# Attention, two MLPs, one core: no draining steps after the first batch, three buffers for its q and k, splits two steps ahead, M's last rows last in the first x2

## The chip, the cores and the metric

One core of a Trainium2 chip. The metric is device time in microseconds of one execution, the median over runs. TensorE (PE) multiplies matrices into PSUM, VectorE (DVE) and ScalarE (ACT) read PSUM and SBUF, GpSimd (POOL) works on SBUF, and the DMA queue of SyncE (SP) carries the transfers.

## The reference, cut to what matters

4 batches of 8 heads, 576 positions, head size 64; then 2304 rows through two blocks.

```python
scores = scale * np.matmul(q, k.transpose(0, 1, 3, 2))
s_pos = np.maximum(s, 0.0)
cum = np.cumsum(s_pos, axis=-1)
bias = -(cum[:, :, :, None] - cum[:, :, None, :])
scores = np.where(causal, -1000000000.0, scores + np.minimum(bias, 0.0))
attn = softmax(scores)                    # row maximum, exp, sum + 1e-9
x = np.matmul(attn, v)                    # heads side by side: (2304, 512)
a = x @ w1                                # (2304, 1024)
b = x @ w2
x2 = ((a * b) @ w3) @ w_out               # (2304, 512)
h = x2 @ w_in                             # (2304, 1024)
solu = h * softmax(h)
ln = (solu - mean) / sqrt(var + 1e-06) * g_ln
out = ln @ w_out2                         # (2304, 512)
```

## The kernel before

A number that needs more than one pass of TensorE is held as two parts, a high and a low one (`hi`, L90, and `lo`, L96), and a product is three matmuls (high by high, high by low, low by high). The weights come as 64-bit words in pieces of 128 x 512. `stage` loads a piece (two buffers during attention, four later), `to_f32` makes one 32-bit number of the two words (POOL or ScalarE at L369 or L371, then VectorE at L375, L376 and L379), and `split_w` writes the high part on ScalarE and the low part on VectorE or POOL (L97). This is a conversion; `pump(n)` runs n of them from a list.

The first loop goes over steps. Step `st` has a head `h` to score and a head `ph` to finish, two heads behind. Scoring is `qk_part` 0 to 2: matmuls of q and k (`sc`), VectorE adds the mask and takes the row extremes (L205), ScalarE takes the exponential (L209); `normalise` has VectorE take the reciprocals (L236, L237) and POOL scale the rows (L241). Finishing is `tr_part` 0 to 3, transposes by TensorE (L273 to L281) with copies out of PSUM into PT by ScalarE and VectorE in turn (L92, L94), and, for every second head, `av_parts`: attention times v (L305) into the tiles xT of its batch. Heads 0 to 7, the first batch, use plain 32-bit q and k in two pairs of buffers QN and KN (L183); later heads use parts, made by `split_qk` (ScalarE copies to QB and KA, VectorE casts to QA, POOL subtracts for QA and KB), with buffers QB, KB, QA and KA for two heads; L191 and L192 are their matmuls. `load_head` and `load_aug` issue the loads of a head and of its two extra rows on SP.

Before the change the steps are: heads 0 to 7; then two steps that score nothing and finish heads 6 and 7; then heads 8 and 9, which finish nothing; then the rest, 36 steps in all. From step 10 on, units of the first MLP (`ab_unit`: 12 matmuls for a and 12 for b of half a column block, L333, a copy of a by ScalarE, a product by VectorE, L353) are put between the parts of the steps as filling, `NF` of them in a step; the units of a batch need all of its xT. `PUMP` says how many conversions of w1 and w2 a step runs; unit i of a batch needs conversions 2i and 2i + 1. From step 11 on PSUM is dealt out anew. The `av_parts` of pairs up to head 9 run at once at the end of their step, the later ones one step late, among the filling.

Then the last units run, then M = w3 w_out is made row block by row block (`m_unit`, L595, high part MH by ScalarE, low part ML by VectorE) beside the conversions of w_in. Then x2 = g M for chunks of 256 rows: `x2_unit(c, *ms)` takes the column groups ms (of four), for each over the first seven row blocks of M, then over the eighth. The first chunk is done one column group at a time, and four conversions of the second w_out stand between the first and the second group. Then `h_unit`, `tr2` (L727) and `out_unit` follow for 18 tiles of 128 rows.

The order of the instructions on each engine is not that of the program: a planner (`schedule_with_timeline_sim=True`) orders them by the program's order as priority and its own estimate of when each is ready. Each engine then runs its own list in order.

## Time and profile before

| | us |
|---|---|
| median of 3 runs (802.27 to 805.4) | 804.95 |
| the profiled execution, device time | 808.67 |
| its span, first to last instruction | 806.9 |
| TensorE busy | 768.1 |
| VectorE busy | 461.1 |
| ScalarE busy | 350.1 |
| POOL busy | 261.5 |

TensorE's busy time is the time in which at least one matmul is under way; with a lower granted clock the same matmuls take longer, so a stretch is read by busy time and clock together. The mean granted clock was 0.979 of full speed. Busy times of VectorE contain the time in which an instruction was held up after its start. An idle time in brackets is that of the engine just before an instruction, with the instruction that ended it.

### The profile page before, as it was taken

What the parts mean: (1) busy time and instruction counts of PE and PEld (TensorE: products, weight loads), DVE (VectorE), ACT (ScalarE), POOL (GpSimd) and SP (SyncE); (2) the same over time, 40 slices, a digit from 0 to 9 for tenths busy, and PEclk for the clock granted to TensorE, in tenths of its full rate; (3) what the DMA queues carried; (4) which work ended last, traced back from release to release, by engine and by line L of the source; (5) the groups of instructions that cost most, each with busy time, mean ns of one, the idle gap of its engine ahead of it and who ended that gap; (6) DMA issues with size and microseconds to landing.
All of it is one profiled execution on the core that took longest, in us unless ns stands there. A gap on an engine that the chain in (4) does not pass through costs nothing.

```text
span 806.9 us, 13174 instructions
## 1 busy us (share of the span) xinstructions
PE 768.1 (95%) x4864; PEld 656.5 (81%) x4864; DVE 461.1 (57%) x1058; ACT 350.1 (43%) x847; POOL 261.5 (32%) x339
## 2 busy tenths in 40 slices
PE   7998979999999999999989969799999999999997
PEld 4555878788888888898988858788888888888886
DVE  5897698866454444325976899834344243433231
ACT  3763556576555464322435335624233232422231
POOL 8655568876544553102322344400000000000000
PEclk9998999999999999999999979899999999999999
DMA  5633355334323320104658644122020200000001
GB/s 149 179 111 98 114 169 164 106 94 130 87 79 104 90 75 31 45 30 170 239 167 281 210 160 139 72 66 66 14 66 14 66 26 14 14 14 14 14 27 39
DMA packets 38040, 75.59 MB, mean 94 GB/s; under 512 B 6796, under 2 KB 18060, under 8 KB 37976
## 3 DMA queue, kind: packets, MB, share of 16 engines
q1 hardware_dynamic: 37976, 74.76, 30.0%
q8 instruction: 38, 0.62, 0.3%
q14 instruction: 26, 0.21, 0.1%
HBM read 60.36 MB, written 14.38 MB: 93 GB/s over the span
## 4 chain that ended last, share of the span: by engine, by line
PE 72%; DVE 10%; DMA 8%; POOL 4%; issue 3%; ACT 2%; SPq 0%; ACTq 0%; DVEq 0%; POOLq 0%
PE o L738 13%; PE h L689 11%; PE x L669 10%; PE b L333 10%; PE a L333 9%; PE av L305 6%; PE tr L273 4%; DMA stage<-in_w_dram 3%; DVE stage L376 2%; PE sc L183 2%; DVE stage L375 2%; PE tr L727 2%; PE sc L191 2%; PE sc L192 2%; DVE stage L379 2%
## 5 line engine op out<-in xcount | busy, mean ns | idle before, releaser
L209 ACT ACTIVATE P<-P,STAT 64x64 f32<-64x64 f32 (+4 forms) x160 | 88.2, 553 | 58.4 <-DVE STAT L205 56.5
L241 POOL TENSOR_SCALAR P<-P,STAT 128x576 f32<-128x576 f32 (+4 forms) x160 | 89.7, 579 | 31.9 <-DVE STAT L237 29.9
L711 POOL TENSOR_TENSOR sv<-sv,mhalf 128x1 f32<-128x1 f32 x18 | 10.0, 555 | 262.2 <-DVE sv L708 262.2
L669 PE MATMUL x<-gh,MH 128*128 128x256 f32 x288 | 84.0, 292 | 5.8 <-ACT MH L92 5.8
L697 DVE TENSOR_REDUCE sv<-h 128x1 f32<-128x1024 f32 x18 | 22.0, 1224 | 115.1 <-PE h L689 115.1
L205 DVE CUSTOM_DVE_ANT_0 P<-sc,wmask 64x64 f32<-64x64 f32 (+4 forms) x160 | 71.7, 482 | 22.8 <-PE sc L192 13.9
L669 PE MATMUL x<-gh,ML 128*128 128x256 f32 x288 | 82.3, 286 | 2.2 <-DVE ML L97 2.2
L669 PE MATMUL x<-gl,MH 128*128 128x256 f32 x288 | 82.2, 286 | 0.0
L97 POOL TENSOR_TENSOR QA<-qk,QB 64x576 fp32r<-64x576 f32 x24 | 36.0, 1498 | 86.1 <-ACT QB L92 72.8
L333 PE MATMUL b<-xT0h,W 128*128 128x288 f32 x256 | 60.8, 309 | 3.2 <-DVE g_sb L353 3.2
L371 POOL TENSOR_SCALAR stage<-stage 128x512 f32<-128x512 f32 x40 | 32.2, 804 | 95.1 <-PE b L333 37.2
L669 PEld LDWEIGHTS x<-gh,MH 128*128 128x128 f32 x288 | 56.3, 195 | 7.1 <-ACT MH L92 6.3
L333 PE MATMUL b<-xT1h,W 128*128 128x288 f32 x256 | 59.2, 302 | 2.1 <-ACT a_sb L345 1.2
L94 DVE COPY PT<-tr 64x128 f32<-64x128 f32 (+5 forms) x112 | 41.2, 383 | 32.2 <-PE tr L281 11.0
L333 PE MATMUL a<-xT0h,W 128*128 128x288 f32 x256 | 59.2, 304 | 0.0
L689 PE MATMUL h<-IH,x2l 128*128 128x512 f32 x144 | 56.7, 394 | 1.5 <-DVE x2l L97 1.5
L333 PE MATMUL a<-xT1h,W 128*128 128x288 f32 x256 | 58.1, 300 | 0.0
L669 PEld LDWEIGHTS x<-gh,ML 128*128 128x128 f32 x288 | 56.0, 195 | 2.5 <-DVE ML L97 2.4
L353 DVE TENSOR_TENSOR g_sb<-b,a_sb 128x288 f32<-128x288 f32 x64 | 28.8, 452 | 50.9 <-PE b L333 25.3
L305 PE MATMUL av<-PT,vr 64*64 64x64 f32 (+4 forms) x384 | 57.2, 412 | 0.3 <-DVE PT L94 0.3
L738 PE MATMUL o<-OH,lh 128*128 128x512 f32 x144 | 57.1, 397 | 0.4 <-ACT lh L92 0.4
L738 PE MATMUL o<-OH,ll 128*128 128x512 f32 x144 | 57.0, 396 | 0.0
(124 smaller groups left out, 2032.5 us busy)
## 6 DMA issues: line engine op xcount, KB each, us to landing
stage<-in_w_dram SPq DMA_DIRECT2D x32, 512.0 KB
qk<-in_qk_dram SPq DMA_DIRECT2D x48, 288.0 KB
g_scr<-g_sb SPq DMA_DIRECT2D x32, 288.0 KB
stage<-in_wo_dram SPq DMA_DIRECT2D x16, 512.0 KB
graw<-g_scr SPq DMA_DIRECT2D x6, 1024.0 KB
out_dram<-o SPq DMA_DIRECT2D x18, 256.0 KB
vr<-in_vm_dram SPq DMA_DIRECT2D x16, 256.0 KB
stage<-in_w_in_dram SPq DMA_DIRECT2D x8, 512.0 KB
```

Of the source, the lines that this page charges most:

```text
L94: eng.tensor_copy(out=dst, in_=src)
L97: eng.tensor_tensor(out=dst, in0=src, in1=hi_.bitcast(F32), op=ALU.subtract)
L205: nc.vector.tensor_tensor_reduce(out=dst2, in0=ps_in, in1=msk, scale=-SCALE, scalar=BIG, op0=ALU.add, op1=ALU.min, accum_out=st[0:rows, ti ...
L209: nc.scalar.activation(out=dst, in_=dst, func=AF.Exp, bias=st[0:rows, ti:ti + 1], scale=-1.0, accum_out=st[0:rows, 5 + ti:6 + ti],)
L241: nc.gpsimd.tensor_scalar(out=dst, in0=dst, scalar1=r, scalar2=1.0, op0=ALU.mult, op1=ALU.mult)
L273: nc.tensor.transpose(ps[:, c:c + 128], pt[:, QOF[i] + 128 * j:QOF[i] + 128 * j + 128], ident)
L305: nc.tensor.matmul(st["ps"][64 * e:64 * e + 64, 448 + c0:448 + c1], vr[0:rows, j, e], PT[(2 * p + e) % 4][0:rows, o + c0:o + c1], **kw,)
L333: nc.tensor.matmul(ps, w_[:, c, fs], x_[:, c, sl], start=(c == 0 and w_ is WH and x_ is XH), stop=(c == KC - 1 and w_ is WL),)
L371: eng.tensor_scalar(out=high.bitcast(F32), in0=high.bitcast(F32), scalar1=2.0 ** -112, scalar2=1.0, op0=ALU.mult, op1=ALU.mult,)
L669: nc.tensor.matmul(ps[m], w_[:, k, m * 128:m * 128 + 128], g_[:, k], start=(k == 0 and w_ is MH and g_ is GH), stop=(k == KF - 1 and w_ is ...
L689: nc.tensor.matmul(ps[:, hf], x_[:, k, ts_], w_[:, k, hf * 512:hf * 512 + 512], start=(k == 0 and x_ is XH and w_ is IH), stop=(k == KC - ...
L738: nc.tensor.matmul(ps, l_[:, k], w_[:, k], start=(k == 0 and l_ is LH and w_ is OH), stop=(k == KF - 1 and l_ is LL),)
```

## The change

It takes the two steps that score nothing out of the list of steps: head h is scored in step h, head h - 2 finished in it, 34 steps in all. The units are two in each step from 10 on, the conversions are dealt to other steps (16 in all, as before), PSUM is dealt out anew at step 10 instead of 11, and the last pair of every batch is multiplied with v at once. The first batch gets a third pair of q and k buffers, made of a buffer of the tag qk2, set up by VectorE with three memsets and loaded ahead of the first score; a head's load is issued three heads ahead, its split done two heads ahead. In the first x2 all four column groups run together: first seven row blocks of M for all of them, then the eighth, with two of the groups in the halves of a two-bank PSUM tile; the four conversions of the second w_out come after all of it.

```diff
-            nc.sync.dma_start(out=QN[h % 2][64:128], in_=qkT[b, hh, :, 0])
-            after[0] = nc.sync.dma_start(out=KN[h % 2][64:128], in_=qkT[b, hh, :, 1])
+            nc.sync.dma_start(out=QN[h % 3][64:128], in_=qkT[b, hh, :, 0])
+            after[0] = nc.sync.dma_start(out=KN[h % 3][64:128], in_=qkT[b, hh, :, 1])
...
-    WO2 = (0, 4, 0, 0, 0, 2, 2)
-    XMS = ((0,), (1,), (2,), (3,))
+    WO2 = (0, 4, 2, 2)
+    XMS = ((0, 1, 2, 3),)
...
     for i in range(min(NQ, 2)):
         load_aug(i, cum[i:i + 1])
-    if NQ > 2:
-        nc.sync.dma_start(out=cumf_scr, in_=cum)
+
+    qk3 = at.tile([128, 2, S], F32, tag="qk2", bufs=2, name="qk3")
+    QN.append(qk3[:, 0])
+    KN.append(qk3[:, 1])
+    nc.vector.memset(qk3[0:64], 0.0)
+    nc.vector.memset(qk3[0:2, 0], 1.0)
+    nc.vector.memset(qk3[32:34, 1], -1.0)
+    load_head(2)
+    load_aug(2, cum[2:3])
+    nc.sync.dma_start(out=cumf_scr, in_=cum)
...
-    steps = [(h, h - 2 if h >= 2 else None) for h in range(H)]
-    steps += [(None, H - 2), (None, H - 1)]
-    steps += [(h if h < NH else None, h - 2 if h >= H + 2 else None) for h in range(H, NH + 2)]
-    NF = {10: 3, 11: 0, 12: 3, 13: 0, 14: 3, 15: 2, 16: 2, 17: 0, 18: 1, 19: 1, 20: 1, 21: 2, 22: 2, 23: 2, 24: 2, 25: 2, 26: 2, 27: 2, 28: 2, 29: 2, 30: 2, 31: 2, 32: 2, 33: 2, 34: 3, 35: 3}
-    PD, AVO = 10, 2
-    PUMP = {3: 1, 5: 1, 6: 1, 10: 2, 11: 1, 12: 2, 13: 1, 14: 3, 15: 2, 16: 1, 17: 1}
+    steps = [(h if h < NH else None, h - 2 if h >= 2 else None) for h in range(NH + 2)]
+    NF = {st: 2 for st in range(10, NH + 2)}
+    PD, AVO = 8, 2
+    PUMP = {4: 1, 6: 1, 8: 1, 9: 1, 10: 1, 11: 2, 12: 1, 13: 2, 14: 1, 15: 2, 16: 2, 17: 1}
...
-        if st == 11:
+        if st == 10:
             ps_ctx.close()
...
-            if NQ <= h + 2 < NH:
-                load_head(h + 2)
+            if NQ <= h + 3 < NH:
+                load_head(h + 3)
             qk_part(h, 0)
...
-            if h + 1 < NH:
-                split_qk(h + 1)
-            if h < 2 and h + 2 < NQ:
+            if h < 2:
                 aug_rows(QB[h], KB[h])
-            if h + 2 < NH:
-                if h + 2 < NQ:
-                    load_head(h + 2)
-                load_aug(h + 2, cumf_scr[h + 2:h + 3] if h + 2 < NQ else cum_scr[h + 2])
+            if h + 3 < NQ:
+                load_head(h + 3)
+                load_aug(h + 3, cumf_scr[h + 3:h + 4])
+            if NQ <= h + 2 < NH:
+                split_qk(h + 2)
+                load_aug(h + 2, cum_scr[h + 2])
         F(4)
         if ph is not None and ph % 2:
             parts = av_parts(ph // 2)
-            if ph < PD or st == len(steps) - 1:
+            if ph < PD or ph % H == H - 1:
...
-        ps = {m: smalltile("x2")[:, 0:256] for m in ms}
+        if len(ms) == KC:
+            two = bigtile("x2")
+            ps = {m: smalltile("x2")[:, 0:256] if m < 2 else two[:, m - 2, 0:256] for m in ms}
+        else:
+            ps = {m: smalltile("x2")[:, 0:256] for m in ms}
```

## Rows read from the trace of the kernel before

**Rows 1.** The page's totals: engine, busy us (share of the span), instructions.

```profile
PE 768.1 (95%) x4864; PEld 656.5 (81%) x4864; DVE 461.1 (57%) x1058; ACT 350.1 (43%) x847; POOL 261.5 (32%) x339
```

**Rows 2.** Stretches: stretch, length, then PE, PEld, DVE, ACT, POOL busy, clock, DMA, GB/s.

```profile
8.00:57.60 49.60, 44.42 (x221) 27.89 (x222) 39.49 (x128) 32.11 (x99) 32.21 (x55) 0.93 0.54 150
...
57.60:81.00 23.40, 19.60 (x116) 12.06 (x115) 17.02 (x35) 10.31 (x30) 13.27 (x17) 0.85 0.39 117
...
81.00:178.00 97.00, 89.80 (x651) 78.18 (x651) 75.93 (x197) 59.37 (x166) 67.91 (x76) 0.98 0.46 134
...
220.00:260.00 40.00, 40.00 (x300) 34.24 (x299) 18.93 (x65) 20.05 (x58) 18.12 (x25) 1.00 0.37 104
...
460.00:500.00 40.00, 30.55 (x185) 27.66 (x184) 37.13 (x52) 16.70 (x30) 18.52 (x16) 0.87 0.44 143
...
500.00:540.00 40.00, 35.83 (x206) 31.95 (x205) 27.36 (x50) 19.33 (x35) 11.87 (x12) 0.91 0.31 99
```

**Rows 3.** Timeline from 0 to 22: start, us, engine, line, operation, [idle before <-releaser].

```profile
0.88 0.30 DVE L447 MEMSET zz<- 128x288 f32 x1
...
8.13 6.32 PE L183 MATMUL sc<-KN,QN 128*128 128x288 f32 x24 [1.20 <-DMA KN<-cum]
...
9.49 0.76 DVE L205 CUSTOM_DVE_ANT_0 P<-sc,wmask 128x576 f32<-128x576 f32 x1 [2.56 <-PE sc L183]
...
14.60 5.08 POOL L241 TENSOR_SCALAR P<-P,STAT 128x576 f32<-128x576 f32 x10 [0.90 <-DVE STAT L237]
...
16.99 4.87 PE L183 MATMUL sc<-KN,QN 128*128 128x288 f32 x12 [2.54 <-DMA KN<-in_qk_dram]
```

**Rows 4.** Timeline around 37 to 42: POOL, VectorE, TensorE.

```profile
37.01 2.55 POOL L241 TENSOR_SCALAR P<-P,STAT 128x576 f32<-128x576 f32 x5
...
37.07 3.63 DVE L376 SCALAR_TENSOR_TENSOR stage<-stage 128x512 uint32<-128x512 uint32 x1 [1.44 <-POOL stage L371]
...
41.62 1.78 PE L183 MATMUL sc<-KN,QN 128*128 128x320 f32 x4 [2.29 <-DVE PT L94]
```

**Rows 5.** Stretches of line L375 alone: stretch, length, busy (count), clock, DMA, GB/s.

```profile
8.00:57.60 49.60, 2.99 (x5) 0.93 0.54 150
...
57.60:81.00 23.40, 2.71 (x3) 0.85 0.39 117
...
81.00:178.00 97.00, 9.99 (x8) 0.98 0.46 134
```

**Rows 6.** Tile stage, 8 to 180 us: ns min/median/max of VectorE's three lines.

```profile
L375 DVE TENSOR_SCALAR stage<-stage x16: 411/724/3003, 23.2 to 141.9; 128x512 uint32<-128x512 uint32 x16
...
L376 DVE SCALAR_TENSOR_TENSOR stage<-stage x16: 652/677/3631, 24.5 to 145.3; 128x512 uint32<-128x512 uint32 x16
...
L379 DVE SCALAR_TENSOR_TENSOR stage<-stage x16: 673/678/1894, 26.8 to 147.7; 128x512 uint32<-128x512 uint32 x16
```

**Rows 7.** Timeline around 58 to 64, the draining.

```profile
58.37 2.79 DVE L94 CAST QA<-qk 64x576 fp32r<-64x576 f32 x1
...
63.56 0.31 PE L277 MATMUL tr<-ident,P 64*64 64x64 f32 x1 [2.97 <-DVE PT L94]
```

**Rows 8.** Chain that ended last, two steady steps: start, us, engine, what, line.

```profile
203.41 3.15 PE av L305 x24
...
207.36 1.60 PE a L333 x12
...
226.65 3.15 PE av L305 x24
```

**Rows 9.** Timeline of TensorE around 100, in the second batch.

```profile
99.53 0.40 PE L191 MATMUL sc<-KB,QB 128*128 128x288 f32 x1 [0.71 <-POOL KB L97]
...
103.54 0.61 PE L333 MATMUL b<-xT0h,W 128*128 128x288 f32 x1 [3.21 <-DVE g_sb L353]
```

**Rows 10.** Timeline of TensorE around the first x2 and tile 0.

```profile
477.88 0.58 PE L669 MATMUL x<-gh,MH 128*128 128x256 f32 x1 [3.19 <-ACT MH L92]
...
514.61 1.97 PE L727 MATMUL tr<-ident,so 128*128 128x128 f32 x8 [4.17 <-DVE so L712]
```

More of the change, by code (lines that the diff above doesn't have):

```diff
@@ L111, in tile_attention_moe @@
         KO.append(KO[-1] + S - 128 * j)
-    QN = [at.tile([128, S], F32, tag="QA", bufs=2, name=f"QN{i}") for i in range(min(NQ, 2))]
-    KN = [at.tile([128, S], F32, tag="KA", bufs=2, name=f"KN{i}") for i in range(min(NQ, 2))]
+    QN = [at.tile([128, S], F32, tag="QA", bufs=2, name=f"QN{i}") for i in range(2)]
+    KN = [at.tile([128, S], F32, tag="KA", bufs=2, name=f"KN{i}") for i in range(2)]
     PT = [at.tile([128, KO[5]], F32, name=f"PT{i}") for i in range(4)]
@@ L147, in load_aug @@
         if h < NQ:
-            nc.sync.dma_start(out=QN[h % 2][32:33], in_=src)
-            nc.sync.dma_start(out=KN[h % 2][0:1], in_=src)
+            nc.sync.dma_start(out=QN[h % 3][32:33], in_=src)
+            nc.sync.dma_start(out=KN[h % 3][0:1], in_=src)
             return
@@ L183, in qk_mm @@
                 nc.tensor.matmul(
-                    view, QN[h % 2][:, q0:q0 + rows], KN[h % 2][:, c0:c0 + view.shape[-1]],
+                    view, QN[h % 3][:, q0:q0 + rows], KN[h % 3][:, c0:c0 + view.shape[-1]],
                     start=True, stop=True,
@@ L454, in tile_attention_moe @@
     load_head(0)
-    if NQ >= 1:
-        load_head(1)
+    load_head(1)
     cum = at.tile([NH, 2, S], F32, tag="qk2", bufs=2, name="cum")[:, 0]
@@ L467, in tile_attention_moe @@
     for i in range(2):
-        if i < NQ:
-            aug_rows(QN[i], KN[i])
-        if i + 2 >= NQ:
-            aug_rows(QB[i], KB[i])
+        aug_rows(QN[i], KN[i])
     nc.vector.tensor_scalar(out=s_sb, in0=s_sb, scalar1=0.0, scalar2=1.0 / SCALE, op0=ALU.max, op1=ALU.mult)
     nc.vector.tensor_tensor_scan(out=cum, data0=s_sb, data1=zero, initial=0.0, op0=ALU.add, op1=ALU.add)
-    for i in range(min(NQ, 2)):
+    for i in range(2):
         load_aug(i, cum[i:i + 1])
-    if NQ > 2:
-        nc.sync.dma_start(out=cumf_scr, in_=cum)
+    qk3 = at.tile([128, 2, S], F32, tag="qk2", bufs=2, name="qk3")
[7 more added lines that the diff above has]
+    nc.sync.dma_start(out=cumf_scr, in_=cum)
     hi(CK[:, 0], cum, nc.vector)
     lo(CK[:, 1], cum, CK[:, 0])
-    for i in range(NQ, 2):
-        load_aug(i, CK[i:i + 1])
     nc.sync.dma_start(out=cum_scr.bitcast(F32), in_=CK.bitcast(F32))
@@ L492, in tile_attention_moe @@
             nc.gpsimd.memset(t[64:128, KO[j]:KO[j] + 64], 0.0)
-    split_qk(0)
-    if NQ < 1:
-        load_head(1)
     nc.sync.dma_start(out=gln, in_=g_ln.rearrange("(k p) -> p k", p=128))
@@ L809, in tile_attention_moe @@
         if t < 2:
-            wo2_pump(WO2[5 + t])
+            wo2_pump(WO2[2 + t])
         if 0 <= t - 2 < NT:
```

## The prediction

> **What bounds the kernel now.** I read the totals first: TensorE is busy 768.1 of 806.9 us [rows 1], so the change can win only where TensorE stands still or runs slowly. Then the table of stretches: in each I call loss the length less TensorE's busy time times its granted clock [rows 2]. The first batch, 8 to 57.6 us: 49.6 - 44.42 x 0.93 = 8.3 us lost. The draining, 57.6 to 81: 23.4 - 19.60 x 0.85 = 6.7. The second batch up to the last weight conversions, 81 to 178: 97 - 89.8 x 0.98 = 9.0. Between 220 and 260 nothing is lost: TensorE 40.0 of 40 at clock 1.00, VectorE only 18.93. Around the first x2, 460 to 500 and 500 to 540: 13.4 and 7.4 by the same working. So 24 us of loss lie in front and 21 around x2, and in all of them VectorE is busy 68 to 93%: it is the second bound.
>
> Last, the waits. They name VectorE again and again, and behind it POOL: an L376 on VectorE ran 3.63 us from 37.07 while POOL worked on from 37.01 (the median of that line is 0.68), and TensorE stood for 2.29 us until 41.62 [rows 4, 6]. A 2.79 us cast for head 9's split at 58.37 was followed by a 2.97 us wait of TensorE at 63.56 [rows 7]. The orders on the engines are the planner's, not the program's: that cast stood ahead of transposes' copies of step 8, so all below assumes that the planner keeps its manner.
>
> **The change, part by part.** The profiled execution took 808.67 us for a span of 806.9. It is 3.7 us above the median of 804.95; I make the sum in its rows and take it off the median.
>
> *Third q and k.* TensorE scores heads 0 and 1 in 6.32 us (3.16 a head), waits 2.54 us for head 2's load and then takes 4.87 us for it [rows 3]. With a third buffer the load is issued before any score. It removes 2.54 us, and at most 4.87 - 3.16 = 1.71 more. Next late is POOL's normalising of head 0: ten instructions in 5.08 us from 14.60, five done near 17.1, while TensorE would be through with head 2 at 14.45 + 3.16 = 17.6. So it holds: -3.5 us, from -4.2 to 0. Added are three memsets on VectorE. The nearest row, 0.30 us for 288 columns, makes 1152 + 576 + 576 columns 2.4 us; VectorE idles for 2.56 us before its first score row at 9.49 [rows 3], which hides them. Without that cover they would cost their 2.4 us once. SP gets head 2's two loads and two small rows ahead of the two copies of cum; nobody needs those before head 3.
>
> *Fewer conversions in the first batch.* Before, 5 weight conversions had begun by 57.6 us and 8 of the 16 by 81 [rows 5]; the new PUMP asks for 2 in steps 0 to 7 and 4 by step 9. One costs VectorE 0.72 + 0.68 + 0.68 = 2.08 us at the medians [rows 6], some 2.4 with half of the low parts (an estimate: one more pass of 0.68, every second time). Fewer of them mean fewer cases like the one at 37.07, where TensorE has no a and b matmuls to fill with. I take -2 us, the wait of 2.29; from -3 to 0, since the planner may still hoist them.
>
> *No draining steps.* Steps 8 and 9 now score heads 8 and 9 beside the transposes of 6 and 7, without a and b. Two steady steps last 226.65 - 203.41 = 23.24 us [rows 8], 11.62 each, with two units of four matmul groups of 1.60: attention alone is 11.62 - 6.4 = 5.2 us of TensorE. VectorE needs 18.93/40 x 11.62 = 5.5 us a step [rows 2], and 2.4 for its conversion: 7.9. Two such steps are bound by VectorE, 15.8 us for 10.4 of TensorE: 5.4 us lost where 6.7 were. -1.5 us, from -5 to +3 (a further blocked cast as in [rows 7]).
>
> *Steps 10 to 17.* They hold 16 units, two in each, instead of 3, 0, 3, 0, and 12 conversions where 8 stood. VectorE: 5.5 + 1.5 x 2.4 = 9.1 of 11.6 us, 78%; between 81 and 178 it was 75.93 of 97, 78% as well [rows 2]. So I leave the loss as it was, 9 us in some 93. But in steps 15, 16 and 17 the unit needs a conversion pumped in that same step, as steps 10 and 14 did before. The nearest waits are the 0.71 and 3.21 us around 100 [rows 9]: +1 us, from 0 to +9.
>
> *q and k split two steps ahead.* The instructions are the same. The 0.71 us wait for KB at 99.53 [rows 9] goes: -0.7. Added is a wait: split h + 2 writes the buffer of head h, so ScalarE's copy waits for the last score of h in the same step, with the copies out of PSUM and exponentials queued behind it. TensorE issues those scores before the transposes of the step, so it costs nothing while ScalarE (20.05 of 40) has room [rows 2], and up to 0.7 a step in steps 8 and 9 if not. The last pair of a batch is now run at once and not a step late, at two borders: 0, because the other matmuls of the border step cover it; the row of 3.21 [rows 9] bounds it if they don't. Switching PSUM one step number earlier and the retagged buffers cost nothing; the same number of instructions surrounds them.
>
> *M's last rows last.* In the first x2, TensorE waited 3.19 us until 477.88 for the last row of M [rows 10]. 63 matmuls of the other three column groups now come before it, so that wait goes. But VectorE is busy 37.13 of 40 us there [rows 2], and what TensorE waits for next is VectorE: the transposes of tile 0 waited 4.17 us for its last VectorE instruction until 514.61 [rows 10]. None of VectorE's work before that is removed; four conversions only come after the evictions of x2 now. So TensorE arrives early and waits longer: -0.5 us, from -6 to +1.
>
> The sum: -3.5 - 2 - 1.5 + 1 - 0.7 - 0.5 = -7.2 us, 797.8.
>
> A rule speaks against a part of this. The VectorE instruction of 3.63 us ended at 40.70, 1.14 us after POOL's five: about its own 0.68 behind them [rows 4, 6]. The Trainium skill ("SBUF — State Buffer", section "SBUF: two separate sides") says that a VectorE instruction with two SBUF inputs, or in a two-port mode, and a GpSimd instruction exclude each other: whoever starts first holds their shared port pair to its end. The row agrees; by the rule at its worst the sum would be that of the second rival, 816, where the medians, which say that it strikes seldom, give 797.8.
>
> **The rivals.** *VectorE takes it back.* If loss goes with conversions rather than with VectorE's share, 9.0 x 12/8 = 13.5 us are lost in steps 10 to 17, 4.5 more in place of my +1, and the lighter first batch gives nothing (0 for -2): -1.7, some 803. For it: VectorE is at 78% with blocked instructions in it. Against: a and b matmuls fill there. That the planner hoists the conversions as before and so little changes lands there too.
>
> *Slower: conversions held by POOL.* Steps 10 to 17 become bound by VectorE when a conversion costs it over (11.6 - 5.5)/1.5 = 4.1 us. The longest three of its instructions are 3.00 + 3.63 + 1.89 = 8.5 us [rows 6]; half-way between that and the median sum is 5.3, with the low part 5.65: a step takes 5.5 + 1.5 x 5.65 = 14.0 us, 2.4 over, 19 us in eight steps. Less 8.2 from the rest: +11, some 816. For it: POOL is busy 67.91 of 97 us there [rows 2], and steps 15 to 17 have no conversion in hand. Against: L375 took 9.99 us for eight there [rows 5], 1.25 each and 0.53 over its median; were all three lines held as much, a conversion would cost 2.08 + 1.6 + 0.35 = 4.0, still under 4.1.
>
> *More: x2 pays.* If the planner lets tile 0 forward once x2's evictions stand first, the 3.19 us and some of the slow clock behind it (0.87 in 460 to 500, 40 x 0.13 = 5 us of which I give half) come home: -6 more, about 792.
>
> **How the numbers follow.** Forecast 797.8, chance 0.42, own range 793 to 801. More: 0.13. Taken back, or planned as before: 0.25. Slower: 0.20. A measurement of this kernel tells about 0.5%, 4 us, from no change: faster is under 800.9, slower over 809.0. Faster 0.55, same 0.25, slower 0.20. The range takes in 792 below with some room, and half of the slower case: 788 to 812.
>
> **What would show it.** Right: no wait for a q or k load before head 2's scores, and head 7 scored by about 52 us; the first a matmul near 75; VectorE 75 to 85% busy in steps 10 to 17, with TensorE's loss there near 9 us; no wait for M's last row, and a longer wait of the first transposes of tile 0. Wrong: waits of a and b on W in steps 15 to 17, L375 to L379 at means over 1.3 us there, or a loss above 13 us in steps 10 to 17; steps 8 and 9 longer than 20 us together; or waits of TensorE for KA or KB in the steady steps, which would mean that the earlier split waits for its own step.

## The result, and the profile after

The changed kernel took 812.95 us, the median of 4 runs (809.65 to 815.75), against 805.08 for the kernel before beside it: ratio 1.0113, interval 1.0065 to 1.0161. It is slower by 9 us by the ratio, by 7.9 between the medians; the forecast was 7 us faster.

| | before | before, profiled again | after |
|---|---|---|---|
| span of the profiled execution, us | 806.9 | 801.8 | 812.2 |
| mean granted clock | 0.979 | 0.983 | 0.975 |
| TensorE's loss, 8 to 57.6 us | 8.3 | 6.6 | 5.5 |
| 57.6 to 81 | 6.7 | 6.7 | 6.5 |
| 81 to 178 | 9.0 | 8.5 | 14.8 |
| 460 to 500 and 500 to 540 | 13.4, 7.4 | 12.0, 4.3 | 13.2, 7.5 |

Loss is worked out as in the prediction. The second profile of the kernel before shows how far a stretch of one execution can be from the same stretch of another: up to 3.1 us here. The profile of after, totals [rows 1] and stretches [rows 2]:

```profile
PE 774.4 (95%) x4864; PEld 661.5 (81%) x4864; DVE 461.1 (57%) x1061; ACT 350.6 (43%) x847; POOL 269.0 (33%) x339
```

```profile
8.00:57.60 49.60, 45.48 (x239) 28.93 (x239) 43.21 (x132) 33.67 (x105) 34.78 (x60) 0.97 0.54 144
57.60:81.00 23.40, 18.18 (x121) 12.32 (x120) 16.52 (x46) 13.15 (x41) 20.10 (x24) 0.93 0.56 149
81.00:178.00 97.00, 86.51 (x609) 74.72 (x608) 67.36 (x180) 51.58 (x144) 64.07 (x64) 0.95 0.44 129
...
460.00:500.00 40.00, 33.07 (x179) 29.68 (x178) 37.49 (x54) 17.10 (x29) 20.00 (x18) 0.81 0.52 172
500.00:540.00 40.00, 36.57 (x209) 32.32 (x208) 31.38 (x51) 20.82 (x37) 10.89 (x10) 0.89 0.26 79
```

The first batch gained 2.8 us against the first profile of before, 1.1 against the second; the second batch lost 5.8 or 6.3, which is clear of that scatter. There VectorE was not busier but idler: 67.36 of 97 us, 69%, where it had 78%.

The beginning, timeline of after [rows 3]: the memsets cost nothing visible, and head 2 is scored behind head 1 without a wait (3.20 us, done at 17.49).

```profile
5.89 1.02 DVE L476 MEMSET qk<- 64x1152 f32 x1 [0.30 <-DVE cum L469]
...
14.29 3.20 PE L183 MATMUL sc<-qk 128*128 128x288 f32 x12
```

The batch border, timeline of after around 75. The last pair is multiplied with v, ScalarE and VectorE evict it to xT0h and xT0l, and 0.10 us after xT0l is written, at 78.16, TensorE goes on, with head 10's scores at 78.26. The profile names another releaser, POOL's scalings of head 9 (L241), which end in the same time; moving the border, below, speaks for the first. The first a matmul comes at 79.36.

```profile
73.46 3.21 PE L305 MATMUL av<-PT,vr 64*64 64x64 f32 x22 [0.68 <-ACT PT L92]
...
75.99 2.72 POOL L241 TENSOR_SCALAR P<-P,STAT 128x576 f32<-128x576 f32 x5
...
76.72 0.65 ACT L92 ACTIVATE xT0h<-av 128x576 fp32r<-128x576 f32 x1 [2.76 <-PE av L305]
...
77.40 0.76 DVE L97 TENSOR_TENSOR xT0l<-av,xT0h 128x576 fp32r<-128x576 f32 x1 [0.38 <-ACT xT0h L92]
...
78.26 0.37 PE L191 MATMUL sc<-KB,QB 128*128 128x288 f32 x1 [1.59 <-POOL P L241]
...
79.36 0.38 PE L333 MATMUL a<-xT0h,W 128*128 128x288 f32 x1
```

In the kernel before the first a matmul came at 74.31 (72.56 in its second profile), among the last pair's matmuls:

```profile
74.31 0.40 PE L333 MATMUL a<-xT0h,W 128*128 128x288 f32 x1
...
75.69 2.08 PE L305 MATMUL av<-PT,vr 64*64 64x64 f32 x8
```

The conversions [rows 5, 6]: VectorE's three lines from 57.6 to 178 us (line, shapes, count, busy us, mean ns, idle before and what ended it). The means are 0.63, 0.78 and 1.01 us, 2.41 together; before they were 1.15, 0.93 and 0.79, 2.88. So they are not held longer in the mean. But VectorE stood 26.8 us for pieces that hadn't landed; before it was 6.2.

```profile
L379 DVE SCALAR_TENSOR_TENSOR stage<-stage 128x512 uint32<-128x512 uint32 x12 | 12.1, 1011 | 0.1
L376 DVE SCALAR_TENSOR_TENSOR stage<-stage 128x512 uint32<-128x512 uint32 x12 | 9.3, 776 | 4.8 <-POOL stage L371 4.7
L375 DVE TENSOR_SCALAR stage<-stage 128x512 uint32<-128x512 uint32 x12 | 7.5, 625 | 26.8 <-DMA stage<-in_w_dram 26.8
```

The last line in the kernel before:

```profile
L375 DVE TENSOR_SCALAR stage<-stage 128x512 uint32<-128x512 uint32 x11 | 12.7, 1154 | 6.4 <-DMA stage<-in_w_dram 6.2
```

Single ones are held, and at the start of the second batch a conversion stands ahead of the softmax on VectorE. The scores that L205 takes at 87.83 were done at 81.48; VectorE had an L376 of 1.78 and an L379 of 1.79 us in its list before it, each beside a POOL instruction, and TensorE's transposes waited 2.00 us, until 88.65, for the row extremes of L205. The granted clock was 0.71 in the mean of 90 to 100 us.

```profile
84.23 1.31 POOL L97 TENSOR_TENSOR W<-stage,W 128x512 fp32r<-128x512 f32 x1
84.30 1.78 DVE L376 SCALAR_TENSOR_TENSOR stage<-stage 128x512 uint32<-128x512 uint32 x1 [0.57 <-POOL stage L371]
...
85.62 1.74 POOL L97 TENSOR_TENSOR QA<-qk,QB 64x576 fp32r<-64x576 f32 x1
...
86.12 1.79 DVE L379 SCALAR_TENSOR_TENSOR stage<-stage 128x512 uint32<-128x512 uint32 x1
...
87.83 0.48 DVE L205 CUSTOM_DVE_ANT_0 P<-sc,wmask 128x320 f32<-128x320 f32 x1
...
88.65 0.45 PE L281 MATMUL tr<-ident,P 64*64 64x64 f32 x4 [2.00 <-DVE STAT L205]
```

The first x2, TensorE's timeline of after [rows 10]: the wait of 3.19 us for the last row of M is gone, and 3.14 us stand before the first h matmul instead, for the high part of x2. The 0.65 and 2.15 us, 18 matmuls in, are for the seventh row block; the first of them was 2.58 us in the kernel before, 18 matmuls in as well, but 0.51 in its second profile.

```profile
472.78 0.38 PE L670 MATMUL x<-gh,MH 128*128 128x256 f32 x1 [0.65 <-ACT MH L92]
475.43 0.58 PE L670 MATMUL x<-gh,ML 128*128 128x256 f32 x1 [2.15 <-DVE ML L97]
492.59 0.79 PE L690 MATMUL h<-IH,x2h 128*128 128x512 f32 x1 [3.14 <-ACT x2h L92]
```

In the kernel before:

```profile
470.39 0.38 PE L669 MATMUL x<-gh,MH 128*128 128x256 f32 x1 [2.58 <-ACT MH L92]
```

### The profile page after: what moved, and what is told of

Read it like the earlier page. It is cut to its first block, busy times and chain, and to the rows that moved or that the text cites. A ratio compares the mean times of both kernels' runs of the same rounds, so it can differ in the third digit from the quotient of the medians.

```text
span 812.2 us, 13160 instructions
## 1 busy us (share of the span) xinstructions
PE 774.4 (95%) x4864; PEld 661.5 (81%) x4864; DVE 461.1 (57%) x1061; ACT 350.6 (43%) x847; POOL 269.0 (33%) x339
## 4 chain that ended last, share of the span: by engine, by line
PE 67%; DVE 11%; DMA 9%; POOL 5%; issue 4%; ACT 2%; SPq 1%; ACTq 0%; POOLq 0%; DVEq 0%
PE o L739 12%; PE h L690 11%; PE x L670 11%; PE b L333 8%; PE a L333 8%; DMA stage<-in_w_dram 6%; PE av L305 4%; PE tr L273 3%; DVE stage L376 3%; PE sc L183 3%; DVE stage L375 2%; DVE stage L379 2%; PE tr L728 2%; DMA stage<-in_wo_dram 2%; PE sc L191 2%
## 5 line engine op out<-in xcount | busy, mean ns | idle before, releaser
L209 ACT ACTIVATE P<-P,STAT 128x192 f32<-128x192 f32 (+4 forms) x160 | 88.3, 554 | 86.2 <-DVE STAT L205 83.7
L241 POOL TENSOR_SCALAR P<-P,STAT 128x576 f32<-128x576 f32 (+4 forms) x160 | 86.2, 562 | 33.0 <-DVE STAT L237 29.9
L205 DVE CUSTOM_DVE_ANT_0 P<-sc,wmask 128x192 f32<-128x192 f32 (+4 forms) x160 | 71.8, 482 | 14.8 <-PE sc L192 10.5
L97 POOL TENSOR_TENSOR QA<-qk,QB 64x576 fp32r<-64x576 f32 x24 | 39.8, 1658 | 82.7 <-ACT QB L92 47.9
L371 POOL TENSOR_SCALAR stage<-stage 128x512 f32<-128x512 f32 x40 | 35.3, 883 | 90.4 <-DMA stage<-in_w_dram 35.7
L690 PE MATMUL h<-IH,x2h 128*128 128x512 f32 x144 | 57.5, 399 | 6.6 <-ACT x2h L92 4.1
L690 PE MATMUL h<-IH,x2l 128*128 128x512 f32 x144 | 57.6, 401 | 1.0 <-DVE x2l L97 1.0
L670 PEld LDWEIGHTS x<-gl,MH 128*128 128x128 f32 x288 | 56.9, 198 | 0.9
L690 PE MATMUL h<-IL,x2h 128*128 128x512 f32 x144 | 57.4, 399 | 0.0
```

The costliest lines, as they stand in the source:

```text
L97: eng.tensor_tensor(out=dst, in0=src, in1=hi_.bitcast(F32), op=ALU.subtract)
L205: nc.vector.tensor_tensor_reduce(out=dst2, in0=ps_in, in1=msk, scale=-SCALE, scalar=BIG, op0=ALU.add, op1=ALU.min, accum_out=st[0:rows, ti ...
L209: nc.scalar.activation(out=dst, in_=dst, func=AF.Exp, bias=st[0:rows, ti:ti + 1], scale=-1.0, accum_out=st[0:rows, 5 + ti:6 + ti],)
L241: nc.gpsimd.tensor_scalar(out=dst, in0=dst, scalar1=r, scalar2=1.0, op0=ALU.mult, op1=ALU.mult)
L371: eng.tensor_scalar(out=high.bitcast(F32), in0=high.bitcast(F32), scalar1=2.0 ** -112, scalar2=1.0, op0=ALU.mult, op1=ALU.mult,)
L670: nc.tensor.matmul(ps[m], w_[:, k, m * 128:m * 128 + 128], g_[:, k], start=(k == 0 and w_ is MH and g_ is GH), stop=(k == KF - 1 and w_ is ...
```

## The experiments

Ratios are to the kernel before, run beside each kernel on the same chip, with 95% intervals. Microseconds beside a ratio are worked out from it; the difference of the medians can be some 1.5 us off them.

### One part at a time

The third buffer alone, on the kernel before:

```diff
-            nc.sync.dma_start(out=QN[h % 2][64:128], in_=qkT[b, hh, :, 0])
+            nc.sync.dma_start(out=QN[h % 3][64:128], in_=qkT[b, hh, :, 0])
...
+    qk3 = at.tile([128, 2, S], F32, tag="qk2", bufs=2, name="qk3")
...
+    load_head(2)
+    load_aug(2, cum[2:3])
```

> The kernel before with the third pair of q and k buffers alone (draining steps, splits and dealing of conversions and units as before). By the prediction -3.5 us, ratio 0.996: head 2 scored by 18 us instead of 22.7. If the gain of the first heads is given back on VectorE before the a and b matmuls begin: ratio 1.000.

Measured 792.65 us, 0.9856 (0.9829 to 0.9883): 1.4%, 11.6 us, faster. The stretches of this kernel, columns as in [rows 2]:

```profile
57.60:81.00 23.40, 22.66 (x144) 15.72 (x145) 18.49 (x38) 11.07 (x29) 14.62 (x14) 0.93 0.33 97
81.00:178.00 97.00, 93.65 (x687) 79.45 (x686) 74.41 (x211) 62.38 (x177) 74.92 (x87) 1.00 0.51 144
```

Loss 23.4 - 22.66 x 0.93 = 2.3 and 3.4 us, where the kernel before had 6.7 and 9.0. So most of the gain comes after the buffer is out of use.

The steps part alone (34 steps, its tables of units and conversions, PSUM at step 10, last pair at once), with two buffers, the split one step ahead and the old x2:

```diff
+    steps = [(h if h < NH else None, h - 2 if h >= 2 else None) for h in range(NH + 2)]
+    NF = {st: 2 for st in range(10, NH + 2)}
...
+        if st == 10:
```

> The kernel before with the steps' part of the change alone (34 steps, two units a step from step 10, the new dealing of conversions, PSUM at step 10, last pair of a batch at once); two buffers, splits one step ahead, the old first x2. By the prediction -1.5 -2 +1, ratio 0.997. By the trace of the changed kernel (conversions dealt to steps 8 to 17 wait there for their loads, 23.1 us of VectorE against 6.2): +4 to +6, ratio 1.005 to 1.008, with the same waits at L375.

Measured 808.21, 1.0047 (1.0022 to 1.0073). That is just below what the trace of the changed kernel had led to expect, and without its waits: VectorE stood 8.2 us for pieces between 81 and 178 us, where the changed kernel had 23.1.

The x2 part alone on the kernel before, and the whole change without it:

```diff
+    WO2 = (0, 4, 2, 2)
+    XMS = ((0, 1, 2, 3),)
```

> The kernel before with the edit of the first x2 alone (all four column groups together, M's eighth row block last, the four conversions behind them). Theory X: +5 us, ratio 1.005 to 1.008, with waits of TensorE in h for x2's high part of 3 us and more where the old form waits for M. Theory F, and my prediction (-0.5 us): ratio 0.998 to 1.001.

> The changed kernel with the first x2 as before the change (one column group at a time, four conversions of the second w_out behind the first group). The traces put 1 us of the 5.3 us between the two spans behind the first batches (from M on): if that is the edit, 1 us less, 812, ratio 1.010. A rival: the edit's late evictions cost as much as TensorE's new waits of 3.1, 1.0, 2.5 and 0.9 us there: 7 us less, 806.

Measured 808.66, 1.0052 (1.0025 to 1.008) with it alone, and 808.5, 1.0048 (1.0011 to 1.0086) for the change without it, against 1.0113 with it. The x2 part costs some 0.5 to 0.65%, 4 to 5 us; the second of these differences is hardly clear of its intervals. TensorE's timeline of the kernel before with the x2 part shows where it stands:

```profile
488.12 0.80 PE L693 MATMUL h<-IH,x2h 128*128 128x512 f32 x1 [6.03 <-ACT x2h L92]
```

All four column groups now end together, and their evictions stand between the last x2 matmul and the first h. From the first x2 matmul to the end of the span the changed kernel took 812.2 - 469.87 = 342.3 us, without the x2 part 805.8 - 469.32 = 336.5. The kernel before was profiled again for this: 336 to 338 us were expected there if the x2 part costs 5 us, 341 if it costs nothing. It took 801.8 - 463.75 = 338.05, but 341.3 in its first profile, and with the x2 part alone 341.9: one execution's end scatters by 3 us, so the ratios carry this reading.

The parts don't add up: -1.44 + 0.47 + 0.52 gives -0.45%, and 1.13% was measured. What the third buffer gives must be lost to another part.

### First theory: the pieces' late loads

VectorE's 26.8 us for pieces were the plainest difference, so I first held them to be the cause. Three kernels on the changed one. Only the first two of the 16 pieces of w1 and w2 are loaded, and the rest of the conversions use them again, so w1 and w2 are not the reference's:

```diff
+        if stg[0] is at and len(kept) == 2:
+            kept.append(kept.pop(0))
+            return kept[-1]
```

> The changed kernel, but of the 16 pieces of w1 and w2 only the first two are loaded; the other 14 conversions run again on these two staging buffers (the numbers are then not those of w1 and w2; every conversion's instructions stay). Theory L (late loads): between 78 and 185 us the changed kernel's VectorE waits 23.1 us in 6 times at L375 for a piece's load (6.2 us in 4 times before the change), with the softmax of the heads behind it in its order; without the loads these waits are 0, TensorE's loss in 78 to 185 falls from about 15 us to 9 or less, and the time comes to about 805, ratio to the kernel before 1.00. Theory C (conversions too dense, or held by POOL): nothing changes but the loads, so 811 to 813, ratio 1.01.

Measured 810.95, 1.0081 (1.0056 to 1.0105). No wait for a piece was left, and the loss from 81 to 178 us was 97 - 93.42 x 0.96 = 7.3 us, half of what it was; but that from 57.6 to 81 rose to 23.4 - 16.60 x 0.65 = 12.6:

```profile
57.60:81.00 23.40, 16.60 (x78) 10.58 (x78) 22.34 (x53) 14.10 (x39) 20.28 (x20) 0.65 0.26 65
81.00:178.00 97.00, 93.42 (x673) 79.14 (x674) 62.30 (x177) 53.80 (x151) 57.28 (x65) 0.96 0.31 84
```

The planner drew the conversions forward into the end of the first batch, where VectorE was now busy 22.34 of 23.4 us: 11 of the 16 had begun by 81 us, 6 in the changed kernel. So this run took out the waits and moved the conversions as well.

Three staging buffers instead of two:

```diff
-    stg = [at, 2]
+    stg = [at, 3]
```

> The changed kernel with three staging buffers during attention instead of two, so that a piece is loaded one conversion earlier. Theory L: VectorE's waits for the loads fall from 23 us to under 10, time 805 to 808, ratio 1.00 to 1.004. Theory C: the conversions are as many and as dense, 811 to 813.

Measured 807.22, 1.0037 (1.002 to 1.0054). That is theory L's time, but not by its mechanism: VectorE still stood 17.6 us for pieces between 81 and 178 us, and what fell most was the loss of the first batch, from 5.5 to 49.6 - 48.41 x 1.00 = 1.2 us. The conversions pumped earlier, one a step from step 5:

```diff
+    PUMP = {3: 1, 5: 1, 6: 1, 7: 1, 8: 1, 9: 1, 10: 1, 11: 1, 12: 1, 13: 1, 14: 1, 15: 1, 16: 2, 17: 2}
```

> The changed kernel with conversions dealt one to a step from step 5 to 15 and the rest at 3, 16 and 17 (PUMP 3:1, 5 to 15: 1 each, 16:2, 17:2), so six are asked for by step 9 instead of four. Theory L: pieces still come behind the heads' loads, but never two in one step before 16, so the waits fall by a third to a half: 807 to 810. Theory C: fewer conversions in steps 10 to 17 (10 for 12), loss falls in proportion, 9 x 2/12 = 1 to 2 us: 810 to 812.

Measured 813.39, 1.0114 (1.0083 to 1.0145): nothing. Without any such load the kernel got only 0.3% faster, though its loss had moved elsewhere, so these three don't settle it. The next kernels do: with the split one step ahead these waits halve and the time stays.

### Where the buffer's gain went

The buffer with the steps part, the split one step ahead, old x2; and the buffer with the split two steps ahead, but with the draining steps. The first kernel's split, against the change:

```diff
-            if NQ <= h + 2 < NH:
-                split_qk(h + 2)
+            if NQ <= h + 1 < NH:
+                split_qk(h + 1)
```

> The kernel before with the third q and k buffer and with the steps part (34 steps, its units, conversions and the last pair at once), but q and k split one step ahead and the old first x2. It differs from the steps part alone (808.21, 1.0047) by the buffer, and from the change without its x2 part (808.5, 1.0048) by the split. Theory A, the draining steps were worth more than the buffer can give without them (its gain was a shorter draining and a second batch without waits): the gain of 12 us is lost whatever the split does: 806 to 809, ratio 1.002 to 1.006, and TensorE's loss between 81 and 178 us stays above 11 us. Theory B, the buffer's gain is eaten by the split two steps ahead, which puts the weight pieces' loads behind a later load of q and k: here the gain comes back, 796 to 799, ratio 0.989 to 0.993, VectorE's wait for pieces falls from 23 us to under 10 and the loss to about 6.

> The kernel before with the third buffer and q and k split and loaded one step earlier, the draining steps kept, old first x2. The buffer alone gave 792.65, ratio 0.9856. Theory A (the draining steps hold the gain): the split changes little, 791 to 795, ratio 0.983 to 0.988. Theory B (the split makes the late loads): 800 to 806, ratio 0.995 to 1.002, with VectorE waiting over 15 us for pieces between 81 and 178 us, where the buffer alone had 5.9.

Measured 808.6, 1.0051 (1.002 to 1.0081) and 793.84, 0.9884 (0.9847 to 0.9921). Theory A held both times: taking out the draining steps loses the gain, 1.0051/0.9856 = 2.0% or 16 us, and the split two ahead changes nothing that these intervals tell; with the draining steps VectorE stood 4.9 us for pieces, not over 15. In the first kernel VectorE stood 11.9 us for pieces between 81 and 178 us, in the change without its x2 part (split two ahead) 22.5, at the same time: 1.0051 and 1.0048.

That the density of units and conversions does it was tried with one unit instead of two in four of the steps, and the conversions spread:

```diff
-    NF = {st: 2 for st in range(10, NH + 2)}
+    NF = {st: 1 if st in (10, 11, 12, 14) else 3 if st > 29 else 2 for st in range(10, NH + 2)}
...
+    PUMP = {4: 1, 6: 1, 8: 1, 9: 1, 10: 1, 11: 1, 12: 1, 13: 1, 14: 1, 15: 1, 16: 1, 17: 1, 18: 2, 19: 2}
```

> As the first kernel of this call, but the first units and conversions of the second batch are spread: one unit instead of two in steps 10, 11, 12 and 14, three instead of two in steps 30 to 33, one conversion a step from 10 to 17 and two in 18 and 19. Theory A1, the density of conversions and products on VectorE makes the loss once the draining steps are gone: 3 to 8 us under the first kernel of this call, loss between 81 and 178 us below 9. Theory A2, the loss comes from too little other work for TensorE while softmax and transposes wait for each other, and the draining steps kept the two apart: fewer units there make it no better, within 2 us of the first kernel or up to 6 slower.

Measured 806.41, 1.0025 (1.0003 to 1.0048): 2.2 us better, between the two theories' numbers, and the loss from 81 to 178 us, 97 - 90.10 x 0.93 = 13.2, speaks against A1; what A2 gives as the reason is not tested by it. And three staging buffers with the third buffer alone:

> The kernel before with the third buffer and three staging buffers for the weight pieces in place of two. VectorE waited 9 us for pieces in the kernel with the third buffer. If such waits set TensorE's loss also where the draining steps are kept, as in the whole change (three staging buffers gave it 0.7%), 788 to 791, ratio 0.980 to 0.984; if they are hidden there, since TensorE loses only 3.4 us between 81 and 178, the same 792 to 793 as with the buffer alone.

Measured 799.63, 0.9956 (0.993 to 0.9983), a full per cent slower than with two. Neither expectation had that. In its trace 7 conversions and not 5 had begun by 57.6 us, the first a matmul came at 73.40 and not at 67.91, and the losses from 57.6 to 81 and from 81 to 178 us were 6.5 and 7.4.

### The border at which PSUM is dealt out anew

The trace of the buffer without draining steps gave the lead. Its timeline at the end of the first batch, VectorE, POOL and TensorE:

```profile
74.99 3.13 POOL L241 TENSOR_SCALAR P<-P,STAT 128x576 f32<-128x576 f32 x5
...
76.41 0.64 ACT L92 ACTIVATE xT0h<-av 128x576 fp32r<-128x576 f32 x1
...
78.10 0.63 POOL L371 TENSOR_SCALAR stage<-stage 128x512 f32<-128x512 f32 x1
78.70 1.28 POOL L97 TENSOR_TENSOR W<-stage,W 128x512 fp32r<-128x512 f32 x1
78.76 1.77 DVE L376 SCALAR_TENSOR_TENSOR stage<-stage 128x512 uint32<-128x512 uint32 x1 [2.97 <-POOL stage L371]
...
80.45 0.74 DVE L97 TENSOR_TENSOR xT0l<-av,xT0h 128x576 fp32r<-128x576 f32 x1
...
81.30 0.58 PE L191 MATMUL sc<-KB,QB 128*128 128x288 f32 x1 [4.95 <-issue]
```

TensorE had ended the last pair at 76.35. xT0l, the last eviction from the old PSUM buffers, stood on VectorE behind an L376, which waited 2.97 us for POOL's L371, which stood behind five scalings of head 9. When xT0l was written, at 81.19, TensorE went on, 0.11 us later and with a lower clock (0.71 in the mean of 74 to 82 us). The profile names no releaser; the matmul is the first in the new PSUM buffers. With draining steps and three buffers the same place looks like this:

```profile
67.91 0.40 PE L333 MATMUL a<-xT0h,W 128*128 128x288 f32 x1
...
69.30 2.08 PE L305 MATMUL av<-PT,vr 64*64 64x64 f32 x8
71.31 0.40 PE L333 MATMUL b<-xT0h,W 128*128 128x288 f32 x1
...
71.90 1.50 PE L305 MATMUL av<-PT,vr 128*64 128x448 f32 x8
```

The units of step 10 run among the av matmuls of the last pair, drawn forward by the planner from the next step, because they still use the old PSUM buffers. After the change they don't: a new dealing at step 10 stands between. So I moved that border alone, by one number:

```diff
-        if st == 10:
+        if st == 11:
```

in the buffer without draining steps (and to 13), in the whole change, and the other way round, 11 to 10, in the kernel with the buffer and the draining steps.

> The kernel with the third buffer and without draining steps (split one ahead, old x2: 808.6, 1.0051), with one number changed: PSUM is dealt out anew at step 11, as in the kernel before, and not at step 10. In its trace TensorE stood 4.95 us until 81.30, right after VectorE had written xT0l, the last eviction of pair 3 from the old PSUM buffers, and its first a matmul came at 83.32; with the draining steps and the buffer it came at 67.91, between the av matmuls of pair 3. Theory P, the new dealing is a border that no matmul of step 10 passes before the last eviction of step 9, so the units of step 10 can't be drawn forward into steps 8 and 9: with the border a step later the first a matmul comes before 76, TensorE's loss between 66 and 90 us falls from some 11 us to under 5, and the time to 798 to 803, ratio 0.991 to 0.998. Theory D, steps 8 and 9 without draining are bound by VectorE whatever TensorE has at hand: within 2.5 us of 808.6.

> The same with PSUM dealt out anew at step 13. Theory P: as with step 11, 798 to 803, since the border is out of the way of pair 3; up to 2 us more or less, because steps 11 and 12 then have four small PSUM buffers and not six, and the border stands where the second batch's first pairs are finished. Theory D: within 3 us of 808.6.

> The whole change (812.95, 1.0113) with PSUM dealt out anew at step 11. Theory P: TensorE's wait of 1.59 us until 78.26 goes, the first a matmul (79.36) comes before 76, and the time falls by 4 to 8 us, 805 to 809, ratio 1.001 to 1.007; what stays over the kernel before is the first x2 (4 us) and the late loads of the weight pieces. Theory D: within 2.5 us of 812.95.

> The kernel before with the third buffer (792.65, 0.9856) and PSUM dealt out anew at step 10 in place of 11, the draining steps kept. Theory P: the units of step 10 no longer run among the av matmuls of pair 3; the first a matmul (67.91) comes after 76 and the time rises by 4 to 10 us, 797 to 803, ratio 0.991 to 0.999. Theory D: the draining steps carry the gain and the border costs nothing: within 2.5 us of 792.65.

| kernel | border at | us | ratio (interval) | first a matmul |
|---|---|---|---|---|
| buffer, no draining | 10 | 808.6 | 1.0051 (1.002 to 1.0081) | 83.32 |
| the same | 11 | 802.68 | 0.9993 (0.9974 to 1.0013) | 71.75 |
| the same | 13 | 802.77 | 1.0005 (0.9981 to 1.0029) | 71.1 |
| whole change | 10 | 812.95 | 1.0113 (1.0065 to 1.0161) | 79.36 |
| the same | 11 | 806.42 | 1.0030 (1.0005 to 1.0054) | 75.5 |
| buffer, draining | 11 | 792.65 | 0.9856 (0.9829 to 0.9883) | 67.91 |
| the same | 10 | 798.24 | 0.9949 (0.9918 to 0.9979) | 75.88 |

In the first kernel with the border at 11, the loss from 66 to 90 us came down less than expected, from 10.7 to 7.6 us: the units behind the last pair still wait for its evictions, as its timeline shows.

```profile
81.46 0.40 PE L333 MATMUL a<-xT0h,W 128*128 128x288 f32 x1 [2.15 <-ACT xT0h L92]
...
83.52 0.61 PE L333 MATMUL a<-xT0l,W 128*128 128x288 f32 x1 [1.52 <-DVE xT0l L97]
```

Otherwise theory P held, in sign and place, in all three pairs: the border directly behind the last pair costs 0.6 to 0.9%, 5 to 7.5 us. In the last pair the border was moved up and nothing else, and the wait appeared where it should, with the unit behind it. xT0h was written at 71.25; xT0l stood behind conversions on VectorE and was written at 74.25, and here the profile names it as the releaser:

```profile
70.60 0.65 ACT L92 ACTIVATE xT0h<-av 128x576 fp32r<-128x576 f32 x1 [3.31 <-PE av L305]
...
71.86 1.13 DVE L379 SCALAR_TENSOR_TENSOR stage<-stage 128x512 uint32<-128x512 uint32 x1
...
72.91 0.68 DVE L376 SCALAR_TENSOR_TENSOR stage<-stage 128x512 uint32<-128x512 uint32 x1
...
73.51 0.74 DVE L97 TENSOR_TENSOR xT0l<-av,xT0h 128x576 fp32r<-128x576 f32 x1
...
74.31 0.40 PE L191 MATMUL sc<-KB,QB 128*128 128x288 f32 x1 [3.76 <-DVE xT0l L97]
```

In the whole change the loss from 81 to 178 us fell from 14.8 to 97 - 91.09 x 0.98 = 7.7 us, while VectorE still stood 16.8 us for pieces there (23.1 with the border at 10): half of that loss was the border's, and most of the loads' waits stayed without it.

```profile
81.00:178.00 97.00, 91.09 (x659) 78.61 (x659) 69.80 (x183) 52.74 (x147) 69.80 (x76) 0.98 0.45 136
```

### What is left of it

With the border back at 11, the kernel without draining steps still stands 0.9993/0.9856 = 1.4%, 11 us, over the one with them. In both, VectorE's three instructions of each conversion of w1 and w2 are left out, so that these weights are only the scaled high words:

```diff
+        if stg[0] is at:
+            return high.bitcast(F32)
         nc.vector.tensor_scalar(out=low, in0=low, scalar1=29, scalar2=None, op0=ALU.logical_shift_right)
```

> The kernel without draining steps, with the third buffer and with PSUM dealt out anew at step 11 (802.68, 0.9993), in which the three VectorE instructions of each of the 16 conversions of w1 and w2 (L375, L376, L379) are left out, so that w1 and w2 are only the scaled high words; loads, POOL's scaling and the split stay. That takes 16 x 2.08 = 33 us of VectorE's work from the stretch before 180 us. To be compared with the next kernel. Theory V, what the draining steps were worth is room on VectorE for these conversions: without them this kernel comes to within 4 us of the next. Theory C, it is the chain of the batch's end (scores, softmax and transposes of heads 8 and 9 stand between the last pair and the units that need it, whatever VectorE has to do besides): the gap stays at 8 to 11 us. Both: the kernel itself gets faster, 786 to 796.

> The kernel before with the third buffer (792.65, 0.9856) and the same instructions left out. Theory V: it gains little, since its conversions already fit (loss of 3.4 us between 81 and 178 us, 2.3 between 57.6 and 81): 786 to 790, ratio 0.978 to 0.983, within 4 us of the kernel without draining steps. Theory C: the same 786 to 790, and 8 to 11 us under the kernel without draining steps.

Measured 787.4, 0.9777 (0.9747 to 0.9806) without draining steps, and 784.11, 0.9728 (0.9701 to 0.9755) with them (a little under what both theories expected): 0.5% apart, 3 to 4 us, where it was 11. By the two intervals the difference is an estimated 0.1 to 0.9%. That is theory V's number. The stretches, first without, then with draining steps:

```profile
57.60:81.00 23.40, 21.62 (x150) 16.65 (x149) 16.39 (x46) 16.24 (x46) 22.41 (x27) 1.00 0.69 195
81.00:178.00 97.00, 94.28 (x689) 81.67 (x688) 48.56 (x152) 53.13 (x150) 50.15 (x62) 0.98 0.41 116
```

```profile
57.60:81.00 23.40, 22.30 (x158) 18.48 (x159) 11.68 (x38) 11.80 (x31) 10.10 (x15) 1.00 0.46 140
81.00:178.00 97.00, 95.88 (x717) 82.67 (x716) 59.20 (x190) 65.16 (x190) 70.61 (x87) 1.00 0.47 132
```

Losses 1.8 and 4.6 us against 1.1 and 1.1. So about two thirds of the 11 us hang on VectorE's part of the conversions. That the draining steps gave them room is the reading that fits; it is not shown by itself. The draining steps went together with other tables of units and conversions and with the last pair multiplied at once, and no run takes these apart with the border at 11; and where TensorE loses as little as here, another difference on VectorE would have shrunk too. With VectorE's share of the conversions gone, what it does and what it waits for go together; these runs don't tell the two apart. The last 3 to 4 us stay open; that the a and b matmuls have to wait for the last pair until heads 8 and 9 are through is argued, not shown.

## Why the prediction was wrong, point by point

**Third buffer, -3.5 us: right in its row, far too small.** Head 2's wait went and its scores took 3.20 us, as worked out. Alone the buffer gave 11.6 us. The step that failed is that it summed the stall and stopped there: a batch that ends earlier sets a and b going earlier (67.91 for 74.31), and the losses of the next two stretches fell by 10.0 us in the profiles (6.7 to 2.3 and 9.0 to 3.4). With the border at 10, which holds the first a matmul back to 75.88, the buffer kernel keeps 0.5%, 4.1 us, of it; so most of the rest hangs on a and b running early. The kernel before, without the buffer, was not run with that border.

**Fewer conversions in the first batch, -2: hardly came about.** The planner drew them forward, as the range allowed for: 4 and not 2 had begun by 57.6 us (5 before), 6 by 81 (8 before). With 5 and 9, when they are pumped earlier, the time was the same (1.0114 against 1.0113).

**No draining steps, -1.5, and steps 10 to 17, +1: this is where the sign turned.** In the presence of the third buffer both together cost 16 us. Three steps of the working failed. "Switching PSUM one step number earlier [...] cost nothing; the same number of instructions surrounds them" priced a border by counting instructions; it costs 5 to 7.5 us, because with it a step later a and b matmuls of the next step fill the batch's end. "So I leave the loss as it was" took VectorE's share, 78%, for the limit. The share fell to 69% and the loss rose to 14.8 us, for VectorE's list is run in order: L205 stood behind a conversion at 84.30 in the changed kernel, and xT0l behind one in the kernels with the buffer and the border at 10. With the border moved the loss was 7.7, less than the 9.0 before; that such stands count only where the border leaves TensorE nothing else to do is argued. And the draining steps were priced at what TensorE loses in them, 6.7 us, not at what they give: with VectorE's part of the conversions gone they were worth 7 us less, so it is likely room for these, which is argued. Head 7 was scored by 54.15 us (forecast 52; 57.64 and 56.09 in the two profiles of before) and head 10's first scores began at 78.26, so steps 8 and 9 took 24 us; the limit named was 20.

**q and k split two ahead, -0.7: nothing either way.** With draining steps 0.9884 against 0.9856, without them 1.0048 against 1.0051. Without draining steps it doubled VectorE's waits for pieces (11.9 to 22.5 us from 81 to 178 us), which I hadn't priced, and which cost nothing that was measured; with them it didn't (5.9 and 4.9).

**M's last rows last, -0.5 (to +1): wrong, +3 to 5.** The lower figure is for x2 and split together with the border at 11 (1.0030 against 0.9993). The step that failed is the place of the next wait. That the wait moves was right; it moved to x2's own evictions before the first h (3.14 us in the changed kernel, 6.03 with that part alone), and not to tile 0's transposes.

**The rivals.** "VectorE takes it back" put the loss in steps 10 to 17 at 13.5 us, and it was 14.8 from 81 to 178; that matches in size, but its reason, loss in proportion to the conversions, doesn't: with the border moved it was 7.7 at the same number of conversions. "Slower: conversions held by POOL", 816, came nearest in time, but its price is refuted: a conversion cost VectorE 2.41 us in the mean, not over 4.1, so the nearness in time is luck. Single places of it were real. In the kernel with the buffer and without draining steps an L376 at 78.76 ran 1.77 us beside a POOL instruction of 78.70 to 79.98 and ended 0.55 us behind it. That agrees with the rule of the Trainium skill ("SBUF — State Buffer", section "SBUF: two separate sides") that the two exclude each other; 1.1 us of the 4.95 hang on it. In the changed kernel the L376 and L379 from 84.30 on ended 0.54 and 0.55 us behind theirs, ahead of TensorE's wait of 2.00 us. "More: x2 pays" failed.

By the runs, each part on top of the ones named before it, the sum is: buffer -11.6, no draining with its tables +11.0, the border +4.7, the split -0.2, x2 +5.2, together 9.1, and 812.95 x (1 - 1/1.0113) = 9.1 was measured. Added in a row like this the parts must give the whole, so the sum is no further proof; in another order they have other prices, as the steps part with 0.47% without the buffer and 2.0% with it. The third buffer alone, 792.65 us, beats both kernels.

## What to carry to other kernels

An edit that moves a border, a new dealing of PSUM or anything that no instruction is drawn across, is priced by what ran across it before: look in the trace for work of the next step among that of the last. A stretch with stalls may be the room that something else uses, so ask what before closing it; and an engine that runs its list in order can hold up the chain at 69% busy, so its share alone doesn't price a stretch. Time each part alone and in combination: here the best part's gain was lost to its neighbour.

## What was not expected of the hardware

At two places a stand of TensorE cost more in its clock behind it. In the kernel with the buffer and without draining steps, after the 4.95 us until 81.30 the first 128x288 matmul took 0.58 us, where it took 0.40 at full clock, and the mean granted clock was 0.71 from 74 to 82, which contains the stand, and 0.80 from 82 to 90 us, a part of each at the lower level of 1.2 GHz; with the buffer and the draining steps it was 1.00 throughout. In the changed kernel TensorE stood 3.3 us from 82 to 90 us; from 90 to 100 it stood 0.1 us, but the granted clock was 0.71 and it lost 3.0. And three staging buffers made the changed kernel 0.7% faster but the one with the third buffer 1.0% slower; why was not followed up.
